# A new written-out order of operations in a fused recurrence and two-layer kernel: 956 operations placed again

## The chip, the cores and the metric

The kernel runs on one core of one Trainium2 chip. A core has five engines that each run their own instructions in program order: TensorE (PE, matrix products), VectorE (DVE), ScalarE (ACT), GpSimd (POOL) and SyncE (SP), which here only issues transfers. Data lies in SBUF; TensorE writes to PSUM, which has eight banks. The metric is the device time of one launch in microseconds (us), as the median of several runs. Each time in this document comes from those runs or from a profiled execution of the program on the chip.

## What is computed

A gated linear recurrence per batch and head, and then two matrix layers with a squared sine between them:

```python
def _attn_ref(q, k, v, f_logit):          # 4 batches, 8 heads, 768 steps, width 48
    f = 1.0 / (1.0 + np.exp(-f_logit))
    for t in range(S):
        state = f[:, :, t, :, None] * state + np.einsum('bhd,bhe->bhde', k[:, :, t], v[:, :, t])
        y[:, :, t] = np.einsum('bhd,bhde->bhe', q[:, :, t], state)

def _moe_ref(x, w_in, w_out, alpha):      # x: 3072 x 384 (y with heads joined); d_ff = 2048
    h = x @ w_in
    s = np.sin(alpha * h)
    g = h + s * s / (alpha + 1e-09)
    return (g @ w_out).astype(np.float32)
```

## The kernel before

**Tiles.** Time is cut into six chunks of 128 steps. A unit `u` (0 to 11) is the pair of loads, products and exponentials for 256 rows: units 0 to 3 take the first two chunks of one batch each, units 4 to 11 one chunk of two batches each (units 4 and 5 are chunk 2, 6 and 7 chunk 3, and so on). For each unit four blocks of 384 KB are loaded: f, k, q and v (`load`, L259). ScalarE makes the logarithm of the gate from f (exp L342, ln L351), TensorE sums it over time (L360, L366), and ScalarE takes exponentials G and Gi of the sums (L374, L377). k times Gi and q times G (L384, on POOL or VectorE) are then transposed on TensorE (L415) and copied out of PSUM (L461 for units 0 to 3, L584 later), or transposed by a transfer that SP issues (L587, chunks 4 and 5). v is cast to bf16 (L354).

**Attention of a unit.** `attend_two` (units 0 to 3) and `attend` (later) form the scores (L468, L550), mask them on VectorE (L473, L554), and add to y the part inside the chunk (L485, L565) and the part from the state (L490, L559). The state is renewed with products of k and v (L498, L570), a sum (L576) and a decay (L419). `x_of` copies y (L427), transposes it on TensorE (L431, L435, L438) or by a transfer on SP (L445), and so fills x for the layers.

**Layers.** w_in and w_out come in four blocks of 768 KB each (L290, L312) into three staging buffers (`wst`), and are folded with alpha into bf16 weights, two folds a block (L297 on VectorE; L320 on VectorE or L318 on ScalarE for w_out). The fold of w_in takes alpha from a PSUM bank that TensorE fills (`spread`, L293), and the bank is free after the block's second fold. For chunk 0 the first layer runs in halves of 256 tokens (`first_half`, L639), later in 512 tokens (`first`, L620). Each product goes through a sine on ScalarE (L605) and an addition on VectorE (L608), which frees its PSUM banks and gives g. The second layer (`columns`, L657) sums 16 blocks of g into one bank per 128 tokens, is copied out by VectorE or ScalarE (L663) into one of four `osb` buffers, and is stored by SP (L667). An `osb` buffer is free when its store has landed.

**What sets the order.** Every operation is recorded first, with its possible engines and planned costs (`op`). `ORDER` (L21) then lists all 956 in the order in which they are written into the program. A number's value modulo 2000 is the operation; the thousands choose which of its engines it runs on, the ten thousands and millions the PSUM banks that it takes, and the hundred thousands how many idle products TensorE does ahead of it (L705). `in_order` decodes this and gives every other buffer the place that has been free longest. Since each engine works in program order, ORDER fixes every engine's own sequence, and SP's too: a transfer whose buffer is not free holds up all transfers behind it. ScalarE needs two tables, one for exp and ln and one for sine; a load of the other table (L703) is put in where ORDER changes from one to the other. Idle products keep TensorE working at the start, where it has nothing else.

The emitting loop, and where the order is read:

```python
    for o, e, idle in in_order(ops):
        if o.table and o.table != now:
            now = o.table
            nc.scalar.preload_act_table_set(now)
        for _ in range(idle):
            nc.tensor.matmul(banks[:, o.takes[0].place, :], zeros[:, :P], zeros, start=True, stop=True)
        o.emit(e)
```

Of the kernel before, what the change touches and what calls it, by code (L numbers as in the profile page):

```python
# [17 lines left out]

ORDER = [2, 78, 79, 700081, 6, 60082, 140, 3, 141, 83, 2088, 84, 4, 10, 202, 203, 89, 240143, 86, 85, 5, 120095,  # L21
    14, 70000, 30091, 1, 96, 97, 92, 2098, 2080, 144, 6070105, 8, 93, 7, 94, 145, 2087, 100099, 90, 146, 20102,
    106, 147, 70062, 107, 63, 40205, 2152, 20206, 100, 2148, 103, 51, 150, 1000101, 2040104, 120153, 240, 241,
    108, 109, 208, 154, 207, 2214, 2113, 64, 130050, 65, 2110, 360157, 2151, 2155, 158, 9, 50111, 70114, 156,
    2160, 53, 2112, 55, 243, 2142, 2115, 60244, 2149, 245, 159, 40164, 52, 70054, 20161, 60134, 165, 59, 246,
    2252, 162, 5000167, 10137, 2040163, 5010166, 135, 66, 168, 15, 16, 12, 138, 11, 171, 2175, 57, 119, 169,
    136, 20176, 56, 69, 2172, 30058, 139, 40173, 120, 60125, 121, 2177, 2174, 126, 61, 170, 13, 70122, 20184,
    2251, 60, 40178, 123, 10181, 247, 2067, 179, 250, 72, 127, 193, 50116, 2068, 117, 30190, 180, 194, 124, 75,
    60199, 2211, 118, 18, 2213, 195, 40131, 182, 185, 17, 132, 183, 70128, 186, 50716, 2070, 717, 196, 133,
    10187, 71, 191, 20706, 212, 192, 200, 22, 201, 707, 188, 40726, 718, 189, 708, 709, 727, 30736, 209, 197,  # L30
    198, 737, 728, 719, 60257, 2248, 10219, 220, 129, 130, 19, 2073, 258, 259, 253, 20, 260, 2204, 222, 254,
    2210, 70215, 216, 218, 738, 739, 2074, 217, 710, 720, 2076, 310, 311, 255, 221, 721, 729, 256, 740, 23,
    60223, 349, 226, 24, 2242, 77, 741, 742, 224, 26, 730, 731, 227, 722, 723, 27, 60313, 60314, 743, 315, 316,
    264, 2249, 320, 732, 733, 711, 30, 724, 21, 744, 317, 3050229, 7060225, 1020228, 350, 265, 25, 261, 230,
    712, 34, 233, 231, 2318, 2234, 2321, 262, 713, 2734, 40352, 20353, 232, 2237, 6070267, 2714, 20263, 2010266,
    10323, 324, 354, 355, 268, 271, 359, 2275, 2322, 272, 70238, 2239, 2360, 745, 30336, 20235, 2236, 269,
    40273, 276, 325, 10375, 337, 2274, 270, 356, 29, 277, 60326, 376, 338, 40286, 2357, 20290, 327, 420, 421,
    362, 40287, 377, 28, 363, 60378, 20291, 364, 278, 20279, 35, 288, 379, 60294, 292, 289, 2319, 2312, 280,
    60295, 38, 40282, 40283, 293, 281, 296, 20298, 299, 31, 297, 284, 302, 20303, 2361, 60306, 40307, 285,
    50776, 777, 778, 779, 2422, 300, 304, 301, 2351, 308, 40766, 305, 20333, 735, 780, 334, 781, 457, 30346,  # L40
    423, 60424, 20746, 767, 426, 347, 747, 2428, 30328, 425, 309, 526, 458, 768, 329, 782, 60365, 330, 348, 339,
    725, 783, 769, 32, 770, 30380, 42, 381, 366, 33, 2784, 2432, 748, 60385, 771, 2429, 2382, 527, 70341, 340,
    50367, 430, 431, 30454, 386, 368, 342, 2343, 749, 331, 10445, 369, 446, 60460, 332, 60461, 715, 335, 358,
    447, 427, 50433, 434, 750, 435, 36, 455, 772, 751, 559, 2459, 773, 463, 50383, 344, 462, 467, 2774, 2345,
    10370, 752, 371, 384, 753, 560, 60448, 2468, 436, 40416, 417, 754, 37, 437, 418, 20400, 401, 449, 419, 388,
    60389, 70450, 402, 60438, 40404, 40405, 451, 390, 403, 466, 20392, 60393, 464, 439, 391, 396, 452, 406, 456,
    387, 2465, 397, 394, 2440, 70372, 407, 40408, 60409, 398, 40, 395, 20412, 60442, 39, 373, 374, 46, 399,
    20413, 41, 70816, 817, 410, 441, 2528, 818, 414, 819, 820, 47, 411, 40562, 20563, 479, 415, 565, 10482, 564,
    821, 20529, 483, 649, 480, 453, 775, 822, 823, 2469, 484, 20530, 470, 2569, 443, 2570, 40796, 471, 472, 797,
    798, 481, 50756, 532, 531, 2536, 624, 757, 2571, 799, 485, 4561, 49, 20473, 758, 759, 486, 60475, 800, 801,  # L50
    2537, 487, 488, 2824, 10556, 760, 761, 582, 762, 763, 549, 2489, 650, 825, 444, 2567, 490, 474, 476, 70491,
    557, 764, 802, 20786, 533, 803, 2477, 2804, 787, 788, 2538, 30546, 478, 589, 492, 2558, 60583, 40550, 625,
    789, 547, 790, 493, 10585, 2568, 584, 755, 791, 792, 586, 793, 2566, 2587, 590, 44, 30579, 60510, 785,
    60511, 2534, 591, 48, 794, 20552, 43, 494, 551, 512, 60495, 40506, 553, 496, 588, 60507, 2554, 580, 513,
    60518, 20502, 651, 795, 508, 40519, 503, 520, 497, 498, 539, 509, 572, 20499, 40806, 50856, 504, 521, 807,
    60652, 653, 505, 808, 809, 810, 500, 2535, 811, 812, 655, 813, 501, 814, 20627, 60628, 857, 858, 555, 540,
    541, 654, 60573, 40836, 837, 859, 838, 574, 629, 657, 630, 20514, 20515, 542, 2659, 860, 516, 543, 60522,
    2544, 20523, 765, 45, 517, 658, 10826, 839, 4626, 656, 827, 828, 829, 575, 861, 830, 831, 576, 634, 524,
    525, 577, 832, 548, 815, 2632, 667, 631, 862, 863, 660, 20668, 60661, 840, 841, 581, 846, 847, 848, 849,
    850, 833, 805, 842, 662, 669, 633, 2834, 635, 642, 60643, 20636, 843, 10663, 664, 2864, 851, 50670, 2665,  # L60
    852, 853, 671, 644, 844, 10645, 2672, 578, 545, 60596, 646, 637, 60597, 598, 40638, 20616, 639, 647, 60617,
    854, 592, 20593, 640, 40604, 618, 605, 599, 865, 673, 594, 619, 595, 60600, 20620, 20621, 886, 606, 622,
    601, 666, 607, 10876, 602, 40608, 20609, 887, 623, 610, 641, 648, 603, 20612, 611, 60613, 614, 615, 877,
    878, 888, 60678, 679, 680, 879, 880, 881, 882, 883, 40690, 20674, 20691, 889, 681, 835, 855, 890, 891, 692,
    20675, 892, 676, 893, 894, 895, 677, 884, 60694, 885, 20695, 696, 697, 866, 867, 868, 869, 870, 20682,
    60683, 60686, 10896, 897, 693, 898, 899, 687, 684, 685, 40946, 845, 50916, 688, 947, 871, 948, 689, 20698,
    20699, 872, 873, 900, 901, 700, 902, 903, 701, 60926, 70906, 927, 874, 928, 20702, 60703, 929, 907, 908,
    917, 949, 950, 2904, 918, 919, 909, 910, 951, 952, 911, 875, 704, 705, 10936, 930, 953, 905, 2954, 955, 937,
    920, 912, 913, 2914, 921, 915, 938, 931, 932, 933, 2934, 922, 935, 923, 939, 940, 2924, 941, 942, 943, 925,
    2944, 945]  # L70

SLOTS = dict(f=3, k=3, q=3, v=3, lf=2, qk=6, vb=4, gl=6, Gi=2, tr=4, at=3, xT=2, yn=4, s=3, g=18, G=2, osb=4, sum=2,
             wst=3, st0=2, st1=2, st2=2, st3=2)
# [39 lines left out]
def kernel(  # L113
# [19 lines left out]
    B, H, S, D = q.shape  # L133
# [18 lines left out]
    PE, ACT, DVE, POOL, SP = "PE", "ACT", "DVE", "POOL", "SP"  # L152
# [10 lines left out]
    def op(engs, emit, deps=(), takes=(), holds=(), table=None, dma=None, after=0):  # L163
        o = Op(engs, emit, [d for d in deps if d is not None], list(takes), table, dma, after)
        o.uses = set(takes) | set(holds)
        for b in o.uses:
            b.users.append(o)
        ops.append(o)
        return o
# [78 lines left out]
    def load(u, n):  # L248
        b = bufs[n, u] = Buf(n)

        def emit(e):
            if u < B:
                dst = at(b).rearrange("c (h j) d -> c h (j d)", j=2)
                src = srcs[n][u * H:(u + 1) * H, :2 * C, :].rearrange("h (c j) d -> c h (j d)", j=2)
            else:
                c, bp = divmod(u, NU)
                dst = at(b)
                src = srcs[n][bp * 2 * H:(bp + 1) * 2 * H, c * C:(c + 1) * C, :].rearrange("b c d -> c b d")
            engine[e].dma_start(out=dst, in_=src)  # L259
        b.ready = op({SP: 500}, emit, takes=[b], dma=1240 if u < B else 1930)  # L260

    bufs, made = {}, {}

# [18 lines left out]
    def w_in(n):  # L282
        b, pb = Buf("wst"), Buf("ps")
# [13 lines left out]
            nc.vector.tensor_tensor(w_in_bf[:, :, fs][:, :, hs], view()[:, :, hs],  # L297
                                    ps(pb, TOK)[:, hs].unsqueeze(1).to_broadcast([P, KB, TOK // 2]), Alu.mult)
        m = op({PE: 216}, spread, takes=[pb], after=7000)
        l = op({SP: 500}, ld, takes=[b], dma=2350)  # L300
        for h in range(2):
            w_in_made[2 * n + h] = op({DVE: 910}, lambda e, h=h: fold(e, h), deps=[l, m], holds=[b, pb])

    def w_out(n):
        b = Buf("wst")
# [8 lines left out]
        def fold(e, h):  # L314
# [4 lines left out]
            else:  # L319
                nc.vector.tensor_tensor(w_out_bf[:, g0:g0 + 2, :], view()[:, 2 * h:2 * h + 2, :],  # L320
                                        al_r[:, g0:g0 + 2].unsqueeze(2).to_broadcast([P, 2, d_model]), Alu.mult)
        l = op({SP: 500}, ld, takes=[b], dma=2350)
        for h in range(2):
            w_out_made[2 * n + h] = op({DVE: 911, ACT: 1175}, lambda e, h=h: fold(e, h), deps=[l, w_ready["out"]],
                                       holds=[b])
# [325 lines left out]
    def columns(c, t, ms, n):  # L651
# [14 lines left out]
            row = (2 * c + t // 2) * S + t % 2 * C if c < 2 else t * S + c * C  # L666
            nc.sync.dma_start(out=out[row:row + C, ms], in_=at(sbuf)[:, :n])  # L667
        v_ = op({DVE: 150 + n, ACT: 170 + 5 * n // 6}, ev, deps=[prev], takes=[sbuf], holds=[ob])
        op({SP: 400}, store, deps=[v_], holds=[sbuf], dma=3 * n // 2)


    alpha()
# [64 lines left out]
```

## Time and profile before

| | |
|---|---|
| median of 6 runs | 184.47 us (183.21 to 185.52) |
| the profiled execution | 185.52 us |
| its span, first to last instruction | 183.8 us |
| TensorE busy | 173.5 us (94%) |
| VectorE, ScalarE, POOL busy | 138.1, 124.7, 64.9 us |
| loads of f, k, q, v | 48 of 384 KB, median 5.0 to 5.7 us from issue to landing |
| loads of w_in, w_out | 4 and 4 of 768 KB, 8.5 and 7.1 us |
| stores | 23 of 192 KB and 2 of 96 KB |

In the profile's lines, "PE" is a matrix product and "PEld" the loading of its weights, which overlaps. A group's line reads: line of the code, engine, operation, what it writes and reads, shape, count; then the busy time in us and the mean of one in ns; then the engine's idle time before it and what ended that. In a table of stretches a row is: from and to, length, then busy time (and count) of PE, PEld, DVE, ACT and POOL, the clock granted to TensorE as a share, the share of time in which the 16 DMA engines were busy, and GB/s. In the slices of the page each digit is the busy share of a fortieth of the span, in tenths. In the chain, a line is: start, length, and what ran or was waited for. In a timeline a line is: start, length, engine, line of the code, operation, count, and in brackets the idle time before it and what ended it.

### The profile page before, as it was taken

The page shows a single profiled execution, that of the slowest core. Times are in us where ns is not written, and L with a number is a line of the kernel's source. Part 1 is how long each engine was busy: PE and PEld are TensorE (multiplying, and loading weights), DVE is VectorE, ACT ScalarE, POOL GpSimd, SP SyncE. Part 2 cuts the span into 40 slices and gives each one's busy share as a digit, 9 for nine tenths or more (in the row PEclk, how much of TensorE's full clock was granted, in tenths as well). Part 3 has the DMA queues.
Part 4 walks back from the last instruction along what each step waited for, and adds up shares of the span by engine and source line. Part 5 has one row for each costly group of instructions (what it writes and reads, how often), then busy time and mean ns, then how long its engine had stood idle before and what let it go on. Part 6 is the DMA issues. An engine that isn't in the chain of part 4 may idle for free.

```text
span 183.8 us, 4393 instructions
## 1 busy us (share of the span) xinstructions
PE 173.5 (94%) x1772; PEld 106.9 (58%) x1773; DVE 138.1 (75%) x187; ACT 124.7 (68%) x170; POOL 64.9 (35%) x107
## 2 busy tenths in 40 slices
PE   6588899999897999999999999999999999999993
PEld 2356578866584446774556764455665445555562
DVE  4698899899877997979998878867677875474300
ACT  2879799599696979788789547797124672624312
POOL 7468203950396014906737651049300000000000
PEclk9999999999999999999999999999999999999999
DMA  5999999999899999999999969889832400120204
GB/s 148 325 319 347 360 281 279 278 370 223 171 181 180 227 228 225 215 223 203 228 191 173 221 146 201 176 186 164 172 79 46 128 0 4 43 86 0 86 25 150
DMA packets 103516, 33.48 MB, mean 182 GB/s; under 512 B 96684, under 2 KB 101948, under 8 KB 103496
## 3 DMA queue, kind: packets, MB, share of 16 engines
q1 hardware_dynamic: 103440, 33.17, 75.5%
q8 instruction: 14, 0.23, 0.6%
q14 instruction: 6, 0.05, 0.1%
q10 hardware_dynamic: 56, 0.03, 0.1%
HBM read 25.20 MB, written 4.72 MB: 163 GB/s over the span
## 4 chain that ended last, share of the span: by engine, by line
PE 64%; DMA 20%; DVE 6%; SPq 4%; ACT 2%; POOL 2%; issue 1%; DVEq 0%; ACTq 0%; POOLq 0%
PE banks L620 28%; PE banks L657 27%; DMA wst<-in_moe_w_in_dram 5%; DMA k<-in_k_dram 4%; DMA v<-in_v_dram 4%; DMA q<-in_q_dram 4%; SPq L259 3%; DVE w_in_bf L297 3%; DMA out_dram<-osb 2%; DMA f<-in_f_logit_dram 2%; PE banks L550 2%; PE banks L565 2%; PE banks L559 1%; PE banks L415 1%; PE banks L360 1%; POOL qk L384 1%
## 5 line engine op out<-in xcount | busy, mean ns | idle before, releaser
L657 PE MATMUL banks<-w_out_bf,g 128*128 128x384 bf16 (+1 forms) x400 | 71.7, 320 | 0.1
L608 DVE SCALAR_TENSOR_TENSOR g<-s,banks 128x1024 bf16<-128x1024 f32 (+1 forms) x56 | 57.7, 1064 | 11.5 <-ACT s L605 11.0
L605 ACT ACTIVATE s<-banks 128x1024 f32<-128x1024 f32 (+1 forms) x56 | 49.3, 903 | 24.0 <-PE banks L620 22.3
L620 PE MATMUL banks<-xT,w_in_bf 128*128 128x512 bf16 x240 | 56.5, 379 | 0.0
L657 PEld LDWEIGHTS <-g 128*128 128x128 bf16 x400 | 36.5, 98 | 22.4 <-issue 0.4
L620 PEld LDWEIGHTS <-w_in_bf 128*128 128x128 bf16 x240 | 22.4, 98 | 23.1
L384 POOL TENSOR_TENSOR qk<-q,G 128x384 bf16<-128x384 f32 x19 | 19.3, 1017 | 23.4 <-PE banks L657 11.1
L384 POOL TENSOR_TENSOR qk<-k,Gi 128x384 bf16<-128x384 f32 x20 | 20.8, 1047 | 6.6 <-PE banks L498 2.3
L554 DVE TENSOR_TENSOR at<-banks,mask 128x1024 bf16<-128x1024 f32 x16 | 19.1, 1219 | 3.1 <-PE banks L550 2.7
L354 POOL CAST vb<-v 128x768 bf16<-128x768 f32 x9 | 7.7, 863 | 26.7 <-DMA v<-in_v_dram 26.6
L663 ACT COPY osb<-banks 128x384 f32<-128x384 f32 (+1 forms) x14 | 6.3, 459 | 13.5 <-PE banks L657 13.5
L342 ACT ACTIVATE f<-f 128x768 f32<-128x768 f32 x12 | 10.1, 845 | 5.9 <-DMA f<-in_f_logit_dram 5.9
L427 ACT CAST yn<-banks 128x384 bf16<-128x384 f32 x17 | 7.9, 479 | 6.8 <-PE banks L565 6.6
L415 PE MATMUL banks<-ident,qk 128*128 128x128 bf16 x128 | 10.4, 219 | 1.9 <-POOL qk L384 1.0
L419 POOL TENSOR_TENSOR st<-sum,gl 128x384 bf16<-128x384 f32 x11 | 10.0, 908 | 5.8 <-DVE sum L576 4.1
L703 ACT ACT_TABLE_LOAD x9 | 11.5, 1283 | 0.2
L639 PE MATMUL banks<-xT,w_in_bf 128*128 128x256 bf16 x96 | 11.3, 273 | 0.0
L663 DVE COPY osb<-banks 128x384 f32<-128x384 f32 x11 | 6.1, 554 | 6.6 <-PE banks L657 5.2
L374 ACT ACTIVATE G<-banks 128x776 f32<-128x776 f32 (+1 forms) x12 | 9.8, 815 | 0.8 <-POOL gl L380 0.5
L351 ACT ACTIVATE lf<-f 128x768 bf16<-128x768 f32 x12 | 10.2, 846 | 0.2
L473 DVE TENSOR_TENSOR at<-banks,two 128x1024 bf16<-128x1024 f32 x8 | 9.5, 1219 | 0.9 <-PE banks L468 0.8
L415 PEld LDWEIGHTS <-qk 128*128 128x128 bf16 x128 | 8.0, 98 | 3.6 <-POOL qk L384 1.2
(93 smaller groups left out, 188.3 us busy)
## 6 DMA issues: line engine op xcount, KB each, us to landing
f<-in_f_logit_dram SPq DMA_DIRECT2D x12, 384.0 KB, 5.4
k<-in_k_dram SPq DMA_DIRECT2D x12, 384.0 KB, 5.7
q<-in_q_dram SPq DMA_DIRECT2D x12, 384.0 KB, 5.0
v<-in_v_dram SPq DMA_DIRECT2D x12, 384.0 KB, 5.4
out_dram<-osb SPq DMA_DIRECT2D x23, 192.0 KB, 2.3
wst<-in_moe_w_in_dram SPq DMA_DIRECT2D x4, 768.0 KB, 8.5
wst<-in_moe_w_out_dram SPq DMA_DIRECT2D x4, 768.0 KB, 7.1
xT<-yn SPq DMA_TRANSPOSE x12, 2.3
```

The lines of the kernel that those rows point to most:

```text
L342: nc.scalar.activation(out=at(fb_), in_=at(fb_), func=Act.Exp, scale=-1.0)
L351: nc.scalar.activation(out=dst, in_=src, func=Act.Ln, bias=1.0)
L384: engine[e].tensor_mul(at(qkb)[:, x, :, :, :D].rearrange("c p r d -> c (p r) d"), heads(at(src), u, i), g[:, i, :H * D].rearrange("c (h d) ...
L415: nc.tensor.transpose(ps(tpb, 1024, BF16)[:, (x * HP + p) * C:(x * HP + p + 1) * C], at(qkb)[:, x, p, :, :].rearrange("c r e -> c (r e)"), ...
L554: nc.vector.tensor_mul(at(atb).rearrange("c r p t -> c (r p) t"), ps(ab, 1024).rearrange("c (x t) -> c x t", t=C), mask.unsqueeze(1).to_br ...
L605: nc.scalar.activation(out=at(sb)[:, :n], in_=ps(hb, n), func=Act.Sin, bias=QUARTER)
L608: nc.vector.scalar_tensor_tensor(take(at(gb)), at(sb)[:, :n].rearrange("p (j t) -> p j t", j=2), -1.0, ps(hb, n).rearrange("p (j t) -> p j ...
L620: nc.tensor.matmul(ps(hb, 2 * TOK)[:, j * TOK:(j + 1) * TOK], w_in_bf[:, kb, f * P:(f + 1) * P], at(xb)[:, :, kb, :], start=(kb == 0), sto ...
L639: nc.tensor.matmul(h[:, j, :], w_in_bf[:, kb, (fb + j) * P:(fb + j + 1) * P], at(xb)[:, ts, kb, :], start=(kb == 0), stop=(kb == KB - 1))
L657: nc.tensor.matmul(ps(ob, n), at(bufs["g", c, fb])[:, j - fb, t * P:(t + 1) * P], w_out_bf[:, j, ms], start=(j == 0), stop=(j == FB - 1))
L663: (nc.scalar.copy if e == ACT else nc.vector.tensor_copy)(at(sbuf)[:, :n], ps(ob, n))
L703: nc.scalar.preload_act_table_set(now)
```

## The change

ORDER is replaced as a whole. The operations are the same 956, with the same inputs and results. What differs is their sequence on each engine and in SP's queue, the engine of some of them, the PSUM banks, and the number of idle products. Five planned transfer costs in the records change too; they were used when the order was searched, and the program that is emitted does not contain them.

```diff
-ORDER = [2, 78, 79, 700081, 6, 60082, 140, 3, 141, 83, 2088, 84, 4, 10, 202, 203, 89, 240143, 86, 85, 5, 120095,
-    14, 70000, 30091, 1, 96, 97, 92, 2098, 2080, 144, 6070105, 8, 93, 7, 94, 145, 2087, 100099, 90, 146, 20102,
...
+ORDER = [2, 78, 79, 6, 5, 80, 150000, 140, 1, 141, 60081, 40082, 83, 40143, 84, 3, 4, 60144, 2088, 300095, 145,
+    89, 146, 96, 86, 85, 97, 98, 60091, 92, 2094, 7, 10, 2087, 8, 14, 93, 3020105, 106, 240102, 90, 51, 202,
...
-        b.ready = op({SP: 500}, emit, takes=[b], dma=1240 if u < B else 1930)
+        b.ready = op({SP: 500}, emit, takes=[b], dma=1280 if u < B else 1980)
...
-        l = op({SP: 500}, ld, takes=[b], dma=2350)
+        l = op({SP: 500}, ld, takes=[b], dma=2130)
...
-        l = op({SP: 500}, ld, takes=[b], dma=2350)
+        l = op({SP: 500}, ld, takes=[b], dma=2790)
...
-        op({SP: 400}, store, deps=[v_], holds=[sbuf], dma=3 * n // 2)
+        op({SP: 400}, store, deps=[v_], holds=[sbuf], dma=250)
```

Decoded, SP's queue begins as follows (f0 is f of unit 0, in3 the fourth block of w_in, out0 the first of w_out, st a store):

```
before: f0 f1 k0 q0 f2 v0 f3 q1 k1 in3 in0 v1 in1 in2 out0 k3 q3 q2 k2 out1 v2 out2 out3 f4
        v3 f5 k4 q4 k5 q5 f6 k6 f7 v4 v5 f8 st v6 q6 k8 f9 k7 st st q7 f10 v7 st q8 v8 q9 k9 ...
after:  f0 f1 v0 k0 q0 k1 f2 q1 f3 in0 v1 in3 in2 k2 q2 in1 q3 k3 out0 out1 out2 out3 v2 f4
        v3 f5 k4 q4 f6 k5 q6 v5 v4 q5 st st f7 k9 st f8 k6 f9 st v6 f10 v7 q7 k7 q9 v8 q8 ...
```

How many operations of a kind, where a choice exists, stand on which engine:

| operation | before | after |
|---|---|---|
| copy of transposed q, k, units 0 to 3 (L461) | VectorE 13, ScalarE 3 | 8, 8 |
| second layer's eviction (L663) | VectorE 11, ScalarE 14 | 13, 12 |
| k or q product (L384) | POOL 39, VectorE 9 | 38, 10 |
| cast of v (L354) | POOL 9, ScalarE 2, VectorE 1 | 8, 3, 1 |
| fold of w_out (L318, L320) | ScalarE 6, VectorE 2 | 4, 4 |
| copy of y (L427) | ScalarE 17, VectorE 7 | 18, 6 |
| copy into x (L435, L438) | ScalarE 8, VectorE 4 | 5, 7 |
| decay of the state, units 4 on (L419) | POOL 11, VectorE 1 | 9, 3 |

Idle products: 16 before, 12 after. Changes of ScalarE's table: nine in both.

## The prediction

> **What bounds the kernel now.** I read the page's busy shares and slices first, then busy time by stretches of my own choosing, then TensorE's timeline around its idle places, then the chain, and last the groups with shapes kept apart. The page:
>
> ```profile
> PE 173.5 (94%) x1772; PEld 106.9 (58%) x1773; DVE 138.1 (75%) x187; ACT 124.7 (68%) x170; POOL 64.9 (35%) x107
> ...
> PE   6588899999897999999999999999999999999993
> ...
> DMA  5999999999899999999999969889832400120204
> ```
>
> TensorE is the bound except in the first five slices; the DMA engines are full for the first 24. The stretches (length, then busy time by engine) price this. The cut at 22.95 is where the first product of the first layer starts.
>
> ```profile
> 0.00:22.95 22.95, 17.76 (x254) 10.47 (x256) 17.21 (x38) 16.63 (x24) 13.44 (x42) 1.00 0.99 300
> 22.95:45.40 22.45, 22.32 (x268) 17.10 (x264) 21.62 (x35) 20.08 (x36) 9.10 (x11) 1.00 1.02 289
> 45.40:60.00 14.60, 13.11 (x244) 9.09 (x244) 11.24 (x16) 11.08 (x19) 9.08 (x12) 1.00 0.93 178
> 60.00:110.00 50.00, 50.00 (x513) 30.78 (x513) 44.09 (x55) 39.95 (x50) 24.30 (x33) 1.00 1.02 207
> 110.00:112.00 2.00, 1.56 (x13) 0.71 (x10) 0.83 (x2) 1.97 (x3) 0.95 (x2) 1.00 0.80 189
> 112.00:180.80 68.80, 68.80 (x497) 38.71 (x494) 43.08 (x44) 34.71 (x42) 8.03 (x8) 1.00 0.39 92
> ```
>
> From 22.95 to its last product at 180.80 TensorE has 157.85 us and is idle for 0.13 + 1.49 + 0.44 = 2.06: 155.79 of work. That work is the same after the change, so an order can win only (a) by reaching a given amount of remaining work earlier, and (b) the 2.06. In the second row VectorE is busy 21.62 of 22.45: while w_in is folded and the first layer of the first 512 tokens runs, VectorE is as full as TensorE. The idle places of (b):
>
> ```profile
> 50.35 0.57 PE L485 MATMUL banks<-vb,at 64*128 64x48 bf16 x32 [0.48 <-ACT G L374]
> ...
> 57.27 0.40 PE L415 MATMUL banks<-ident,qk 128*128 128x128 bf16 x4 [1.01 <-POOL qk L384]
> ...
> 111.78 0.33 PE L559 MATMUL banks<-st,tr 128*128 128x96 bf16 x4 [0.44 <-DVE osb L663]
> ```
>
> The chain says what lies behind the longest and what starts the dense part:
>
> ```profile
> 11.82 8.49 DMA wst<-in_moe_w_in_dram
> ...
> 42.67 6.92 DMA k<-in_k_dram
> 49.59 6.50 DMA q<-in_q_dram
> ```
>
> So w_in's first block lands at 20.31 and starts the folds; unit 5's q lands at 56.1, POOL multiplies it until 57.2, and TensorE resumes at 57.27. The prices of VectorE:
>
> ```profile
> L608 DVE SCALAR_TENSOR_TENSOR g<-s,banks 128x512 bf16<-128x512 f32 x16 | 9.9, 682 | 0.0
> L297 DVE TENSOR_TENSOR w_in_bf<-wst,banks 128x768 bf16<-128x768 f32 x8 | 7.5, 948 | 1.2 <-DMA wst<-in_moe_w_in_dram 1.2
> L320 DVE TENSOR_TENSOR w_out_bf<-wst,al_r 128x768 bf16<-128x768 f32 x2 | 2.7, 1330 | 0.8 <-DMA wst<-in_moe_w_out_dram 0.8
> ```
>
> Back to back, start to start, they step 0.60 (add) and 0.86 (fold), read from VectorE's timeline.
>
> [...] SP's loads land in the order of issue, the first ones 1.2 us apart. [...] the w_out fold took 1.72 with POOL busy and 0.95 with POOL idle; the adds kept 0.60 beside POOL. [...]
>
> **The change part by part.**
>
> The five edited transfer costs (1240 to 1280 and so on) go into the operations' records, which the emitting loop never reads. They cost nothing because nothing is issued from them; no cover is involved. Only ORDER acts: the same operations, other places, other engines, other banks.
>
> Idle products: 16 become 12, 0.61 each at the early clock; 4 x 0.61 = 2.4 us of TensorE time before the dense part. I count 0, since TensorE waits there for ScalarE, VectorE and POOL; ends: a gain of 0.6 if one stood in the way, a loss of 1 if the clock rises later (a group of ten products took 1.03 from 9.0 and 0.67 from 12.4, so it rose between). Table loads: nine before and nine after, 0.
>
> Engines: VectorE loses 5 transposed copies (0.41) and one y copy (0.55), and gains 2 evictions (0.55), one q/k product (0.66), 2 w_out folds (1.33), 3 xT copies (0.43) and 2 states (0.6): -2.6 + 1.1 + 0.66 + 2.66 + 1.3 + 1.2 = +4.3 us. Beyond 60 us it has 5.9 idle in 50 and 25.7 in 68.8, which hides its share; before 45 us nothing hides it. POOL loses four operations of about 0.9, ScalarE stays within 0.3.
>
> Loads, by equal bytes in the one SP queue. The first nine are attention loads in both. Twelve transfers of the same sizes precede v1's landing at 21.43 before; now the twelfth is w_in 3, so 21.4, with w_in 0 at 17.6 (where the tenth landed). The first 24 transfers are the same set in both, ending with f of unit 4 at 43.4. Stepping back with v's 1.3 and w_out's 3.0 (36.53 less 33.55), the one run of w_out lands at about 31, 34, 37 and 40, and v of unit 2 at 41.5 instead of 37.86. POOL has it cast by 43.3; the first product that reads it is due at 46.6, so this is hidden, with 3 us of cover; without that it would cost us for us.
>
> Start of the dense part. Unit 1's k comes before unit 2's f, so POOL's four products of unit 1 (14.33 to 18.53 before) can run 10.8 to 15.2. ScalarE then has x of the first 256 tokens at 21.4. But VectorE goes: folds of w_in 0 at 17.6 to 19.3, mask 1.14 to 20.5, wait for w_in 3 until 21.4, two folds to 23.2, mask to 24.35. Behind it TensorE can do two half products (0.66 each), but its next spread needs the bank that the second fold frees at 23.2. It reaches the product that follows the mask at 24.4. By then it has done, against before at 22.95, one kv (0.40), two half products (1.31) and one spread more and one other spread less: 1.71 more. Remaining: 155.79 - 1.71 = 154.08, so with no idle time it would end at 24.4 + 154.1 = 178.5.
>
> Whether it idles. VectorE from 21.4: 6 folds of w_in 5.2, mask 1.1, 2 states 1.0, 16 adds 9.6, 3 copies 1.05, 4 w_out folds 3.6: 21.6, so 43.0. Operation by operation, TensorE asks for each freed bank or g 0.3 to 0.5 us after VectorE has given it (35.2 against 34.9; 40.3 against 39.9; 44.6 against 43.9): no idle time, but thin cover. Then unit 4's k and q (48.5 and 50.5, at 1.95 each after f) meet products due at 53; unit 5's q, second after unit 4's, becomes the sixth after it and lands at 62.2, but its transposes move from 59 to 67.8, so the wait of 1.01 goes and has 4.6 us of cover where it went. Unit 6's k lands at 71.5, two POOL steps to 73, due at 73.9: 0.9 of cover. f of unit 9 lands at 73.4; its exp stands on ScalarE ahead of two y copies due at 75. Next late: x of units 6 and 7 for the fourth chunk goes through SP's transposes, done at 105 to 106.3 against 106: 0 to 0.4. The eviction of the third chunk's t1 waits for the store of the second chunk's t3, queued on SP behind two loads (109.5 to 111 against 109.8): 0 to 0.5, taken by banks still free. SP's transposes behind that have 4 us or more.
>
> I take 1.0 us of idle time in all: 0.2 + 0.3 for the last two and 0.5 for small slips. Ends: 0 and 2.5. Sum: 178.5 + 1.0 = 179.5 against 180.8, -1.3. The tail of 3.0 (eviction, store) is unchanged. The profiled execution took 185.52 with its span of 183.8, so 1.7 lies around it; it was the longest of six, whose median is 184.47. The difference goes onto the median: 184.47 - 1.3 = 183.2.
>
> **Rivals.**
>
> *VectorE becomes the bound from 21.4 to 44 (slower).* Every us that the run above is longer, or that w_in 3 lands later, moves TensorE one for one past 0.3 us of cover. Four w_out folds instead of two stand in it; each costs 0.77 more when POOL is reading (1.72 against 0.95), 3.1 for all, and w_in blocks landed up to 2.7 apart, not 2. It decides from 0.3 + 1.3 + 0.9 = 2.5 us. At 3.4 us late: 184.47 - 1.3 + 3.1 = 186.3. For: the 21.62 of 22.45. Against: POOL is nearly idle from 33 to 42, when three of the folds fall.
>
> *The waits only move.* The order removes 2.06 and meets as much at unit 6's k, f of unit 9 and the transposes; a common slip of the loads by 1 us is enough. Then 178.5 + 2.2 = 180.7: 184.4, no change. For: the DMA share is 1.02 from 60 to 110.
>
> *The start is better than I give.* If w_in 3 lands 1 us earlier, VectorE's run starts at 20.5 and idle time stays at 0.8: 178.5 - 0.9 + 0.8 = 178.4, so 182.1. For: three blocks in one stretch landed 2.0 to 2.7 apart.
>
> **How the numbers follow.** The forecast case 0.45 (182.4 to 184.0), the moved waits 0.22 (184.0 to 184.9), the better start 0.14 (181.6 to 182.4), VectorE as the bound 0.19 (185 to 187). 0.5% is 0.92 us, about what a measurement of this kernel tells from no change: faster means under 183.55, which is most of the first case and all of the third, 0.38 + 0.14 = 0.52; same 0.07 + 0.22 = 0.29; slower 0.19. The range 181.7 to 185.6 leaves out most of the slow case and a sliver of the fast one. The faster cases alone: 181.6 to 184.0.
>
> **What would show it.** Right: w_in 3 lands near 21.4; TensorE's last half product of the first chunk is near 39 and its wait at unit 5's q is gone; from 24.4 it idles about 1 us; its last product ends near 179.5. Wrong: idle time on TensorE between 34 and 45 that ends on the add (L608) or a fold (the first rival), or on POOL's k product of unit 6, f of unit 9 or SP's transposes (the second); a clock below 1.00 in the dense part would void the count.

## The result, and the profile after

The changed order takes 183.01 us (median of 16 runs, 181.94 to 186.19) against 184.59 us for the kernel before beside it (median of 37 runs, 182.73 to 186.04). The ratio is 0.9924, with a 95% interval of 0.9899 to 0.9948. The profiled execution took 182.41 us, its span 180.6 us; a part of the longer runs, of both kernels, is left out of every ratio as disturbed.

The page of the kernel after, with engines (busy us, share of the span, instructions) and the slices that were shown of before:

```profile
PE 171.1 (95%) x1768; PEld 105.8 (59%) x1769; DVE 142.1 (79%) x191; ACT 123.8 (69%) x168; POOL 62.3 (34%) x103
...
PE   1699899999999999999999999999999999999993
...
DMA  5999999999999899998999988899731410002114
```

TensorE is busy for 2.4 us less, VectorE for 4.0 us more (the prediction said +4.3) and POOL for 2.6 us less. After the fifth slice TensorE's digits show no dip; before had an 8 and a 7 in the eleventh and the thirteenth. The stretches of the kernel after (from and to, length, then busy us and count of PE, PEld, DVE, ACT and POOL, granted clock, DMA share, GB/s); the first cut, 24.40, stands 0.08 us behind the start of the product that the prediction placed at 24.4:

```profile
0.00:24.40 24.40, 17.85 (x284) 11.32 (x287) 19.64 (x41) 18.40 (x25) 12.78 (x41) 1.00 1.00 294
24.40:45.40 21.00, 21.00 (x240) 16.12 (x241) 20.29 (x31) 18.82 (x35) 9.90 (x13) 1.00 1.03 299
45.40:60.00 14.60, 14.60 (x244) 9.06 (x242) 13.17 (x19) 13.40 (x20) 4.86 (x6) 1.00 1.01 196
60.00:110.00 50.00, 50.00 (x523) 31.03 (x522) 44.54 (x57) 39.78 (x51) 25.77 (x35) 1.00 0.99 201
110.00:177.60 67.60, 67.60 (x494) 38.31 (x490) 44.44 (x47) 33.04 (x39) 8.96 (x9) 1.00 0.42 98
```

In each row from 24.40 on, TensorE's busy time equals the length: the idle places of before are gone and none has come in their stead. The two places that the prediction watched most are unit 5's q and unit 6's k. The timeline of the kernel after, first POOL's product and then the transposes on TensorE that read it, for each:

```profile
62.45 1.00 POOL L383 TENSOR_TENSOR qk<-q,G 128x384 bf16<-128x384 f32 x1
...
67.94 0.83 PE L414 MATMUL banks<-ident,qk 128*128 128x128 bf16 x12
...
73.02 1.00 POOL L383 TENSOR_TENSOR qk<-k,Gi 128x384 bf16<-128x384 f32 x1
...
74.67 0.39 PE L414 MATMUL banks<-ident,qk 128*128 128x128 bf16 x4
```

Unit 5's q is multiplied by 63.45; its transposes, the last third of the group at 67.94, start at 68.38: 4.9 us of cover. Unit 6's k is ready at 74.02 and read at 74.67: 0.65 us. Neither line has an idle time in brackets. The chain of the kernel after, as shares of the span by engine:

```profile
PE 93%; ACT 3%; DMA 2%; issue 0%; DVE 0%
```

It now runs along TensorE nearly from end to end; the three transfers (11.82, 42.67, 49.59) that stood in the chain of before are out of it. VectorE's prices, by shape, after (the fold of w_out had a mean of 1330 ns before, two of them):

```profile
L607 DVE SCALAR_TENSOR_TENSOR g<-s,banks 128x512 bf16<-128x512 f32 x16 | 10.3, 678 | 0.6 <-ACT s L604 0.6
L296 DVE TENSOR_TENSOR w_in_bf<-wst,banks 128x768 bf16<-128x768 f32 x8 | 7.3, 948 | 0.3 <-DMA wst<-in_moe_w_in_dram 0.3
L319 DVE TENSOR_TENSOR w_out_bf<-wst,al_r 128x768 bf16<-128x768 f32 x4 | 3.9, 986 | 0.0
```

The dense part runs from the product behind the mask to the last group of the second layer. Both lines are from TensorE's timeline:

```profile
24.32 0.57 PE L484 MATMUL banks<-vb,at 64*128 64x48 bf16 x32
...
168.04 9.63 PE L656 MATMUL banks<-w_out_bf,g 128*128 128x192 bf16 x74
```

From 24.32 to the end of the last product, 168.04 + 9.63 = 177.67, there are 153.34 us without an idle time. After it come 2.94 us of eviction and store (3.01 before). **This length is the ruler of the experiments below**: what stands ahead of 24.32 varies from one execution to the next, but from there on two executions of after are alike to 0.06 us. In before, whose line numbers are one higher, the same product, with the same 1490 products of TensorE from there on, starts at 24.93, and the last one ends 155.86 us later:

```profile
24.93 0.57 PE L485 MATMUL banks<-vb,at 64*128 64x48 bf16 x32
```

So of the 3.13 us by which TensorE's end moved, 0.61 lie ahead of this product and 2.52 behind it.

### The profile page after: what moved, and what is told of

The parts are those of the page before. It is cut to its first block, busy times and chain, and to the rows that moved or that the text cites. A ratio compares the mean times of both kernels' runs of the same rounds, so it can differ in the third digit from the quotient of the medians.

```text
span 180.6 us, 4390 instructions
## 1 busy us (share of the span) xinstructions
PE 171.1 (95%) x1768; PEld 105.8 (59%) x1769; DVE 142.1 (79%) x191; ACT 123.8 (69%) x168; POOL 62.3 (34%) x103
## 2 busy tenths in 40 slices
DMA packets 103516, 33.48 MB, mean 185 GB/s; under 512 B 96684, under 2 KB 101948, under 8 KB 103496
## 4 chain that ended last, share of the span: by engine, by line
PE 93%; ACT 3%; DMA 2%; issue 0%; DVE 0%
PE banks L656 35%; PE banks L619 29%; PE banks L638 6%; PE banks L414 4%; PE banks L359 3%; PE banks L549 2%; DMA f<-in_f_logit_dram 2%; PE banks L564 2%; PE banks L558 2%; PE banks L704 1%; PE banks L467 1%; PE banks L430 1%; PE banks L569 1%; PE banks L484 1%; PE banks L365 1%; PE banks L292 1%
## 5 line engine op out<-in xcount | busy, mean ns | idle before, releaser
L619 PE MATMUL banks<-xT,w_in_bf 128*128 128x512 bf16 x240 | 55.7, 379 | 0.0
L383 POOL TENSOR_TENSOR qk<-k,Gi 128x384 bf16<-128x384 f32 x21 | 22.0, 1053 | 12.8 <-ACT Gi L376 7.5
L383 POOL TENSOR_TENSOR qk<-q,G 128x384 bf16<-128x384 f32 x17 | 17.6, 1037 | 13.7 <-DMA q<-in_q_dram 7.1
L426 ACT CAST yn<-banks 128x384 bf16<-128x384 f32 x18 | 8.4, 482 | 9.8 <-PE banks L564 9.1
L353 POOL CAST vb<-v 128x768 bf16<-128x768 f32 x8 | 6.6, 824 | 22.1 <-DMA v<-in_v_dram 22.1
L418 POOL TENSOR_TENSOR st<-sum,gl 128x384 bf16<-128x384 f32 x9 | 7.8, 864 | 18.6 <-DVE sum L575 18.6
L662 ACT COPY osb<-banks 128x384 f32<-128x384 f32 (+1 forms) x12 | 5.5, 466 | 11.3 <-PE banks L656 10.8
L662 DVE COPY osb<-banks 128x384 f32<-128x384 f32 (+1 forms) x13 | 6.9, 536 | 6.1 <-PE banks L656 5.9
L702 ACT ACT_TABLE_LOAD x9 | 11.5, 1283 | 0.2
L376 ACT ACTIVATE Gi<-banks 128x768 f32<-128x768 f32 x12 | 9.7, 811 | 2.6 <-PE banks L359 1.6
```

The source lines that it names most:

```text
L383: engine[e].tensor_mul(at(qkb)[:, x, :, :, :D].rearrange("c p r d -> c (p r) d"), heads(at(src), u, i), g[:, i, :H * D].rearrange("c (h d) ...
L619: nc.tensor.matmul(ps(hb, 2 * TOK)[:, j * TOK:(j + 1) * TOK], w_in_bf[:, kb, f * P:(f + 1) * P], at(xb)[:, :, kb, :], start=(kb == 0), sto ...
L662: (nc.scalar.copy if e == ACT else nc.vector.tensor_copy)(at(sbuf)[:, :n], ps(ob, n))
```

## The experiments

The theory: the gain is the idle time of before in the dense part, which the new order takes away because each load now lands ahead of its product. The rivals: the start is earlier; a single part, the one run of w_out, does it; VectorE or a load is about to take the gain back. Each edit is of ORDER alone, and each edited kernel has one profiled execution; "after" is the changed kernel. What was not run is the converse of the load experiments: before with unit 5's q loaded earlier.

### Both kernels again

No edit. The first profile of before came from the longest of six runs, so its 2.06 us of idle time may have been bad luck.

> The kernel before, unchanged, for a second trace. Waits theory (the change gains by taking TensorE's waits out of the dense part, from 22.7 us on): TensorE is idle 1.5 to 2.5 us there, at the same three places (the k and v product's bank at 50, unit 5's q at 57, the eviction at 111), and its first-layer products have a mean over 233 ns. If the idle time is under 0.8 us, the first trace was an unlucky one and the waits cannot carry the whole gain.

> The changed kernel, unchanged, as the base of the runs beside it. Ratio 0.990 to 0.995. TensorE idle under 0.3 us from 22.5 us to its last product; that product ends at 177.5 to 179.

Before took 183.63 us in the run that was profiled; 44 others beside it have a median of 183.96. TensorE's timeline has one idle place left that is longer than 0.15 us in the dense part:

```profile
55.78 0.40 PE L415 MATMUL banks<-ident,qk 128*128 128x128 bf16 x4 [0.97 <-POOL qk L384]
```

Unit 5's q is late again, by nearly the same time (1.01 in the first profile). The 0.48 at unit 1's attention and the 0.44 at the eviction are not there. By stretches TensorE is idle for 0.11 + 0.97 + 0.05 + 0.03 = 1.16 us from 22.09 on, not 2.06, and its last product ends at 178.91, not 180.80. So the first profile was an unlucky one by 0.9 us of idle time, and it started the first layer 0.86 us later too (22.95 against 22.09). The ruler's product starts at 24.07, a length of 154.85 where the first profile had 155.86:

```profile
24.07 0.57 PE L485 MATMUL banks<-vb,at 64*128 64x48 bf16 x32
```

The brackets understate what a wait costs. A product's record runs on past the start of the next one (0.33 us for a product of 384 columns, at a step of 0.16), and idle time is counted only from its end. From start to start of neighbouring products, the four places of the first profile (idle 0.13, 0.48, 1.01 and 0.44) took 0.29, 0.64, 1.12 and 0.61 us more than the usual step there, 2.66 in all; the two over 0.1 in the second (0.11 and 0.97) took 0.27 and 1.09, 1.36 in all.

After was timed again in 22 runs: 182.62 us, ratio 0.9942 (0.9918 to 0.9966). No idle place from 21.4 us on, L484 at 23.93, the last product ends at 177.22: a length of 153.28.

What follows: the wait at unit 5's q is there in both profiles of the old order; the other two places came in one of them. In the second pair of profiles TensorE's end moved by 1.69 us: 0.14 ahead of the ruler's product, 1.57 behind it. Of the 1.57, 1.36 are the two waits and about 0.2 are delays between products that are too short to be listed.

### The loads of one order with the rest of the other

The 56 load entries of ORDER take the sequence of the other kernel; all other entries keep theirs. In SP's queue:

```diff
 after, with the loads of before
-f0 f1 v0 k0 q0 k1 f2 q1 f3 in0 v1 in3 in2 k2 q2 in1 q3 k3 out0 out1 out2 out3 v2 f4 ...
+f0 f1 k0 q0 f2 v0 f3 q1 k1 in3 in0 v1 in1 in2 out0 k3 q3 q2 k2 out1 v2 out2 out3 f4 ...
 before, with the loads of after
-f0 f1 k0 q0 f2 v0 f3 q1 k1 in3 in0 v1 in1 in2 out0 k3 q3 q2 k2 out1 v2 out2 out3 f4 ...
+f0 f1 v0 k0 q0 k1 f2 q1 f3 in0 v1 in3 in2 k2 q2 in1 q3 k3 out0 out1 out2 out3 v2 f4 ...
```

> The changed kernel with the 56 loads in the order of before; every other operation, engine and bank as changed. Waits theory: k and q of unit 2 land at 32 to 34 instead of 24 to 26, and the transposes that stand at 27.8 in TensorE's order wait for them until 35.6: +7 to +9 us. Rival (the order of the engines gains, whatever the loads do): at most +1 us.

> The kernel before with the 56 loads in the changed order; all else as before. Rival (the order of the loads alone carries the gain): -1 to -2 us against the kernel before. Waits theory: the loads meet an order of engines that was made for other times; VectorE's first fold waits for w_in's fourth block until 21.4 instead of 17.6, ScalarE's first w_out fold until 33.5 instead of 29.2: +5 to +7 us.

Measured: 194.46 and 202.8 us, one run each, where before took 183.55 beside them. Both are far slower than either kernel, and by more than expected: some 12 us over after for the first, 19 over before for the second. The waits of TensorE in the first:

```profile
36.27 0.61 PE L414 MATMUL banks<-ident,qk 128*128 128x128 bf16 x4 [6.08 <-POOL qk L383]
37.22 0.61 PE L414 MATMUL banks<-ident,qk 128*128 128x128 bf16 x4 [0.34 <-POOL qk L383]
```

POOL itself stood idle for 11.48 us there until a load of k landed; in the queue of before k2 is the nineteenth transfer, in that of after the fourteenth. The second kernel has four waits of more than 0.4 us:

```profile
22.50 0.33 PE L431 MATMUL banks<-ident,yn 128*128 128x128 bf16 x3 [2.60 <-DVE w_in_bf L297]
...
65.15 0.61 PE L415 MATMUL banks<-ident,qk 128*128 128x128 bf16 x4 [5.14 <-POOL qk L384]
...
112.60 0.40 PE L550 MATMUL banks<-tr 64*128 64x128 bf16 x8 [2.09 <-ACT Gi L377]
...
133.06 2.72 PE L620 MATMUL banks<-xT,w_in_bf 128*128 128x512 bf16 x6 [4.04 <-DVE g L608]
```

What follows: neither half of the change has an effect of its own that could be read off. An order of loads fits one order of products, and the gain belongs to the pair. The idle times of the first make 6.7 us with a last one of 0.24, and L484 starts at 26.72, 2.4 us late; that leaves some 3 of its 12 us, which the last section names.

### The one run of w_out

v of unit 2 goes back between w_out's second and third block, where before had it:

```diff
-out0 out1 out2 out3 v2 f4 ...
+out0 out1 v2 out2 out3 f4 ...
```

> The changed kernel with v of unit 2 loaded between the second and third block of w_out, as before, so that w_out no longer comes in one run. Waits theory: v then lands near 37 instead of 41 and nobody asks for it before 43; w_out's third block lands 1.3 us later, and VectorE's fold of it (38.5) waits 0.3 us at most: 0.0 to +0.4 us against the changed kernel. Rival (the one run of w_out is what gains): it gives back 1 us or more, to a ratio of 0.998 or above.

Measured: 182.82 us, ratio 0.9955 (0.9932 to 0.9977), beside 0.9942 for after on the same chip. No wait in the dense part, length 153.28. So this part of the change is worth nothing that can be measured: the blocks are folded in time either way, and in after v2, cast by 42.46, had 4 us to spare for the product at 46.95 that is due for it.

### How much cover the loads have

Unit 5's q is moved behind two and behind four further loads of 384 KB, and unit 6's k behind v6, f9 and a store:

```diff
 by two
-v5 v4 q5 st st f7 k9 st f8 k6 f9 st v6 ...
+v5 v4 f7 k9 q5 st st st f8 k6 f9 st v6 ...
 by four
-v5 v4 q5 st st f7 k9 st f8 k6 f9 st v6 f10 ...
+v5 v4 f7 k9 f8 v6 q5 st st st k6 f9 st f10 ...
 k6 late
-f8 k6 f9 st v6 f10 ...
+f8 v6 f9 st k6 f10 ...
```

> The changed kernel with q of unit 5 two loads later in the queue (behind f of unit 7 and k of unit 9). It lands 3.8 us later, near 66; POOL's product of it ended at 63.5 and TensorE asked for it at 68.4, a cover of 4.9 us. Waits theory: 0.0 to +0.2 us. Rival (the order is tight here too): +2 us or more.

> The same with q of unit 5 four loads later (also behind f of unit 8 and v of unit 6): 7.7 us later, near 69.8. Waits theory: 7.7 less 4.9 of cover, TensorE waits 2.4 to 3.0 us at unit 5's transposes, and the time grows by as much. Rival (later slack takes it up): under +1 us.

> The changed kernel with k of unit 6 behind f of unit 9, a store and v of unit 6. It lands 4 us later, near 75.4; POOL's product ends at 76.4, TensorE asked for it at 74.7. Waits theory: a wait of 1.3 to 2.0 us at unit 6's transposes and as much time. Rival (slack): under +0.5 us.

| kernel | time, us | ratio to before | length from L484 to TensorE's end | over 153.28 |
|---|---|---|---|---|
| after, again | 182.62 | 0.9942 (0.9918 to 0.9966) | 153.28 | |
| q5 by two | 183.07 | 0.9975 (0.9946 to 1.0005) | 153.28 | 0.00 |
| q5 by four | 185.7 | 1.0091 (1.0063 to 1.012) | 155.34 | 2.06 |
| k6 late | 187.07 | 1.0168 (1.011 to 1.0226) | 157.25 | 3.97 |

By two loads the length is the same to 0.01 us: q5 has more than their time of cover. (The ratio stands 0.3% higher than that of after; its interval overlaps, and the profiled execution lost its time ahead of L484, at 25.05 instead of 23.93.) By four loads the wait of before is back, at the same product and for the same reason. TensorE's timeline of that kernel:

```profile
71.05 0.40 PE L414 MATMUL banks<-ident,qk 128*128 128x128 bf16 x4 [1.83 <-POOL qk L383]
```

From start to start it took 2.00 us more than the usual step, which is the 2.06 of the table. It is shorter than the 2.4 to 3.0 that was expected: POOL began its product 7.55 us later than in after (70.00 against 62.45), nearly as reckoned, but TensorE itself was 0.73 us later (L484 at 25.05 against 24.32). This is the direct test of the theory: q5 too late costs TensorE the wait in full, and with q5 in the place that the change gave it there is none. k6, with 0.65 us of cover, becomes a wait by three places in the queue. But its wait was 2.25 us, where 1.3 to 2.0 was expected, and its price 3.97. TensorE's timeline of that kernel, and below it the stretches around the wait (columns as above):

```profile
77.89 0.40 PE L414 MATMUL banks<-ident,qk 128*128 128x128 bf16 x4 [2.25 <-POOL qk L383]
```

```profile
76.00:78.00 2.00, 0.11 (x2) 0.11 (x3) 0.91 (x2) 0.00 (x0) 1.16 (x2) 1.00 0.73 147
78.00:80.00 2.00, 2.00 (x34) 1.81 (x34) 0.39 (x1) 0.48 (x1) 1.75 (x2) 0.70 1.23 244
80.00:82.00 2.00, 2.00 (x22) 1.49 (x20) 0.66 (x2) 1.44 (x3) 0.07 (x1) 0.50 1.25 217
82.00:84.00 2.00, 2.00 (x27) 1.43 (x25) 1.67 (x4) 2.00 (x3) 0.93 (x1) 0.94 1.37 225
```

The clock column (the third value from the end) falls to 0.70 and 0.50 behind the wait. The 128-wide products step 107 ns apart from about 79 to 82.2 us, and 56 before and after. Some 3.2 us at steps of 107 in place of 56 are 1.5 us lost; from start to start the wait took 2.42 us more than the usual step, and 2.42 + 1.5 = 3.9 is the price but for 0.1. The wait of 1.83 left the clock at 1.00.

### How thin VectorE's cover is

The four folds of w_out that ScalarE does go to VectorE (eight there); and, the other way, the division of before: six block halves on ScalarE, two on VectorE.

```diff
 all eight on VectorE
-2067 2070 2074 2077
+67 70 74 77
 six on ScalarE
-68 73 76 2077
+2068 2073 2076 77
```

> The changed kernel with all eight folds of w_out on VectorE, four more than it has: 4 x 0.95 = 3.8 us more between 33 and 44, ScalarE 4.1 us less. The prediction's step (VectorE is as full as TensorE there, with 0.3 to 0.5 us of cover): TensorE idles 2.5 to 3.8 us between 35 and 46, and the time grows by as much. Rival (VectorE has slack that its order hides): under +0.5 us.

> The changed kernel with w_out's folds divided as before: ScalarE six, VectorE two (the second halves of the second and fourth block). VectorE has 1.9 us less between 33 and 44, ScalarE 2.1 us more. Waits theory: TensorE is not waiting in the changed kernel, so nothing can be gained; ScalarE's sines come up to 2 us later: +0.2 to +1.5 us. Rival (the engines' division costs time on VectorE): -0.3 us or more.

All eight on VectorE: 185.37 us, ratio 1.0101 (1.0078 to 1.0124), length 156.39, 3.1 us more. VectorE got 3.5 us more work (145.6 against 142.1), so all but 0.4 us of it came out on TensorE. Its timeline waits on VectorE where the first rival of the prediction said it would:

```profile
36.29 2.11 PE L656 MATMUL banks<-w_out_bf,g 128*128 128x384 bf16 x12 [1.15 <-DVE g L607]
38.95 0.48 PE L656 MATMUL banks<-w_out_bf,g 128*128 128x384 bf16 x2 [0.55 <-DVE w_out_bf L319]
```

Six on ScalarE: 183.48 us, ratio 0.9995 (0.9974 to 1.0015), length 154.09, 0.8 us more, in waits of 0.18 on ScalarE's fold (36.09) and on VectorE's addition (43.66) and smaller ones. So in this order the even division of the folds is worth 0.8 us against that of before, and 3.1 against all eight on VectorE. Between 34 and 45 us either engine holds TensorE back when it is given the larger share.

### The idle products and the clock

First all twelve idle products are taken out; then nine are put ahead of TensorE's first real product, and none elsewhere:

```diff
 none
-150000 ... 300095 ... 240102 ... 320157 160050 ... 120205 ... 140161
+50000 ... 95 ... 40102 ... 20157 60050 ... 20205 ... 40161
 nine in front
-150000 ... 300095 ... 240102 ... 320157 160050 ... 120205 ... 140161
+950000 ... 95 ... 40102 ... 20157 60050 ... 20205 ... 40161
```

> The changed kernel without its 12 idle products. Prediction's step: they stand in nobody's way, 0 to +0.8 us (TensorE's clock may rise later than near 11 us, which lengthens the products of the start). Rival (idle products hold up the start): -0.6 us.

> Nine idle products of TensorE stand ahead of its first real one, where it has nothing else to do, and the other eleven of the changed order are gone. The run without any idle product showed the clock of TensorE's products rise only at about 20.2 us (128x384 steps of 0.32 to 0.37 us until then, 0.16 after), the changed order at about 11.9. Theory A, the clock is all that idle products give, and they stand in nothing's way: the rise comes by 12 here too, the reach of the third transpose of y (L430) is within 0.5 of 21.2, and the time is within 0.5 us of the changed kernel's (ratio 0.991 to 0.997). Theory B, those from 10 to 21.4 also delay: the same rise, and a start earlier by 0.5 to 1.5 us (ratio 0.986 to 0.991). Theory C, the later ones hold the clock up through the small waits before 21: the rise comes late or is lost again, as without any (ratio 0.997 to 1.001).

Without any: 184.19 us, ratio 0.9989 (0.9953 to 1.0026), against 0.9942 for after on the same chip: 0.0047 x 184 = 0.9 us dearer, with intervals that overlap. Nine in front: 184.0 us, ratio 0.9948 (0.9913 to 0.9982). Both have a dense part of 153.29 us without a wait, so what they lose there lies ahead of it: L484 starts at 26.00 and 25.68, in after at 24.32. (The profile of the first is that of its longest run, 185.63 us; in it the last store also landed 1.7 us later than in the others, which the edit does not explain.) The group of the first unit's transposes shows how. In after, in the kernel without idle products, and in the one with nine in front (of whose group four products stand apart):

```profile
11.31 1.09 PE L414 MATMUL banks<-ident,qk 128*128 128x128 bf16 x16
```

```profile
10.71 1.93 PE L414 MATMUL banks<-ident,qk 128*128 128x128 bf16 x16 [0.20 <-DVE qk L383]
```

```profile
10.82 1.46 PE L414 MATMUL banks<-ident,qk 128*128 128x128 bf16 x12 [0.55 <-DVE qk L383]
```

In after the products of this group step 56 ns, in the other two 107. The change from 107 to 56 is called the rise of the clock here: in the packed traces of after and before the first record of the granted clock, 1.00, begins at 11.37 and 9.79 us, where the steps change. In both of the other two TensorE goes on at the slow step until about 20 us. So nine idle products at the very front, with TensorE busy from 1.26 to 5.28, did not bring the rise forward, and without those from 10 us on it came late both times. That it is these that bring it is likely but not shown: each kernel was profiled once, and in "after, again" below the first of them already ran at the fast step. In its profile the kernel with nine in front went the third way of its expectation, but its time lies in the band of the first: its runs do not tell the theories apart.

The same group shows what differs between executions of one and the same order. Nothing in the order ahead of 24 us differs among the first five of these kernels:

| execution of | first 107 to 56 ns change, about | L484 starts | TensorE ends | length |
|---|---|---|---|---|
| after, again | 9.9 | 23.93 | 177.22 | 153.28 |
| after | 11.4 | 24.32 | 177.67 | 153.34 |
| w_out in two runs | 12.2 | 24.75 | 178.04 | 153.28 |
| q5 by two | 13.7 | 25.05 | 178.34 | 153.28 |
| k6 late | 14 | 25.18 | 182.43 | 157.25 |
| nine in front | 20 | 25.68 | 178.97 | 153.29 |
| no idle products | 20 | 26.00 | 179.29 | 153.29 |

The later the clock rises (9.9 to 20 us), the later the dense part starts (23.93 to 26.00), and that part is then the same (but for k6's wait). Three more executions with the same order ahead of 24 us fit: q5 by four (13.6, L484 at 25.05), eight folds on VectorE (11.1, 23.96) and six on ScalarE (11.5, 24.13). The rest of the spread was there before: the first idle product of this stretch starts between 9.62 and 10.09 us. In both profiles of before the step is already short at 10 us (four transposes in 0.38 from 10.11 and from 9.99): it has seven idle products in front and two more at 8.2. Before reached the ruler's product at 24.07 and 24.93, so after can be up to 1.1 us later or 1.0 earlier there. An order of after with idle products at 8.2 us was not run.

## Why the prediction was right, and where its sum was off

The time, 183.0 against 183.2 predicted, and the verdict (0.76% faster, where faster began at 0.5%) are right, and so is the mechanism: TensorE bounds the kernel, and the order wins mostly by the waits in the dense part (2.52 of 3.13 us in the first pair of profiles, 1.57 of 1.69 in the second). Some of the sum's terms were off, in directions that cancelled, so that an agreement to 0.2 us is in part luck.

**The loads by equal bytes.** Right to 0.6 us nearly everywhere: w_in 0 landed at 17.13 (predicted 17.6), w_in 3 at 21.16 (21.4), f4 42.92 (43.4), k4 48.33 (48.5), q4 50.14 (50.5), q5 62.07 (62.2), f9 72.85 (73.4). Only w_out was off: its first three blocks at 33.48, 35.65 and 37.53 instead of 31, 34 and 37. The first waited on SP for a staging buffer until 28.07. It cost TensorE no wait.

**The start.** 24.32 against 24.4, but not by the path that was reckoned, so this closeness is luck. The step let VectorE decide (w_in 3, folds, mask). In the trace of after the chain runs through ScalarE, whose copy into x TensorE's next transposes wait for, and from 21.21 on through TensorE's own products without a break:

```profile
19.16 0.64 ACT G L373
...
19.88 0.80 ACT Gi L376
20.68 0.49 ACT xT L434
...
21.21 0.33 PE banks L430 x3
```

VectorE's mask was done at 24.14, 0.18 us before the product that reads it:

```profile
22.92 1.22 DVE L472 TENSOR_TENSOR at<-banks,two 128x1024 bf16<-128x1024 f32 x1
```

In "after, again" it was done 0.29 us ahead, with w_out in two runs 0.69. The term that failed is ScalarE's: x of the first 256 tokens was put at 21.4, and the copy that completes it ends at 22.33. The step also counted the idle products at 0 because TensorE waits there for others, with ends of -0.6 and +1. But six of after's idle products, 1.4 us of TensorE's time, lie on this chain between 14 and 24 us, and the clock rises anywhere from 9.9 to 14 us, which moves the start of the dense part between 23.93 and 25.18. The upper end of 1 us was the right size; whether fewer idle products with an early rise would start it sooner was not run.

**The remaining work.** Predicted 154.08, measured 153.28 to 153.34. The term is too large by 0.8. Before takes 1.98 us from its first half product at 22.95 to the ruler's product at 24.93, where 1.71 was taken off (the two half products were put at 0.66 each and take 0.76), which is 0.3. The other 0.5 was waiting that the sum took for work: 155.86 less the 2.06 of listed idle time is 153.80, less the 2.66 counted from start to start it is 153.20.

**The idle time.** Predicted 1.0 (ends 0 and 2.5), measured 0.00, twice. The places were seen rightly as thin: unit 6's k had 0.65 of cover where 0.9 was said, and moving it by three places in the queue did bring the wait. The eviction that stands behind a store did wait, 0.57 us on ScalarE (111.40), and free banks covered it. None of the slips that the term allowed for became a wait.

**The base.** The sum was made against a profile with 2.06 us of idle time; the same kernel profiled again had 1.16. So the gain against that second execution was overstated by about 0.9 us, which the 1.0 of idle time that never came made good, and the 0.8 of overcounted work stood against a start that can come up to 0.8 later than 24.4. Pair by pair, TensorE's end moved from 180.80 to 177.67 in the first profiles and from 178.91 to 177.22 in the second; the medians moved by 1.4 (0.0076 x 184.6) and 1.1 (0.0058 x 184).

**VectorE.** Its work grew by 4.0 us (4.3 predicted) and no wait came of it, as predicted. The cover was given as 0.3 to 0.5; in the trace the addition that ends at 35.31 is read at 35.39, the next two are read 0.14 and 0.19 after they are given. The rival "VectorE becomes the bound" did not come true, but its price was right: it put the cover at 0.3 us and counted one for one beyond it, and with 3.4 us more it gave 186.3 us, 1.0099 of before. With eight folds on VectorE, 3.5 us more work brought 3.1 onto TensorE, and the ratio was 1.0101. Its 2.5 us are the point from which the whole change would have been a loss of 0.5%; waits begin at about 0.4.

**The rivals.** The waits did not move elsewhere. The better start, by a w_in 3 that lands 1 us earlier, did not come either: it landed at 21.16, 0.24 earlier, and VectorE was not what the start waited for.

## What to carry to other kernels

In a kernel that one engine bounds, measure an order by the length from a fixed early product to that engine's last one: where the order has no waits it repeats to 0.06 us while whole runs scatter by 2, and so it shows what an edit costs; with waits it does not (155.86 and 154.85 in before). Profile the kernel before twice before a wait in it is counted as a gain. Count a wait of TensorE from start to start of the products around it, expect that a longer one may cost more than its length (1.83 us of wait cost 2.06 here, 2.25 cost 3.97), and don't judge a new order of loads apart from the order of products for which it was made.

## What the runs showed of the hardware

**A wait can cost nearly double.** In the k6 kernel a wait of 2.25 us cost 3.97. Waits of TensorE of 1.83 and 2.09 us (the second in before with the loads of after) left the clock at 1.00; those of 2.25, 2.60, 4.04, 5.14 and 6.08 were each followed by about 3 to 6 us of products at half speed, for which the clock column shows 0.50. After 2.25 and 2.60 the slow stretch began about 1.1 and 1.5 us behind the wait. Each of these waits was seen in one execution. In after with the loads of before, products ran at half speed from 36.27 to 41.35, which is about 2.4 us lost; its waits, 6.7 us of listed idle time, took 7.15 from start to start, and the two make 9.6 of the 9.7 by which its length (162.99) is over 153.28. In the k6 kernel the slow stretch, 1.5 us lost, is most of the difference to the expectation.

**The rise at the start depends on the execution.** The same instructions ahead of 24 us got the fast clock at 9.9, 11.4 and 12.2 us in three executions: 128 columns took steps of 107 ns before it and of 56 behind it. What sets the moment was not shown. The column of the granted clock shows 1.00 during the slow stretch at the start all the same, since the traces of after and before hold no record of the clock ahead of 11.37 and 9.79 us; there the steps of the products have to be read.
